# Two more banks for batch 1's key features, weight 1's second half first, and a new order of steps on every engine

## The chip, the cores and the metric

The kernel runs on one core of one Trainium2 chip. The metric is the device time of one execution in microseconds; the number for a kernel is the median of its runs.

## The reference

Polynomial-sketch attention over 4 batches, 4 heads, 1088 tokens and 32 features, followed by a block of layer norm, two matrix products and a residual.

```python
def phi(x):                                   # S1, S2: 8 x 32
    a = np.einsum('rd,bhsd->bhsr', S1, x)
    b = np.einsum('rd,bhsd->bhsr', S2, x)
    return np.einsum('bhsi,bhsj->bhsij', a, b).reshape(*x.shape[:-1], 64)
q_p, k_p = phi(q), phi(k)
kv = np.einsum('bhsf,bhsd->bhfd', k_p, v)     # 64 x 32 for each head
z = np.sum(k_p, axis=2)
num = np.einsum('bhsf,bhfd->bhsd', q_p, kv)
den = np.einsum('bhsf,bhf->bhs', q_p, z)[..., None] + 1e-06
x = (num / den) with the heads side by side   # 4 x 1088 x 128
xn = (x - mu) / np.sqrt(var + 1e-06) * g_ln
out = x + np.maximum(xn @ w_ch1, 0.0) @ w_ch2 # 128 -> 512 -> 128
```

The two weights and the sketches arrive as 64-bit floats; the kernel takes their words apart and builds 32-bit floats from them.

## The kernel before

The kernel has no loops over tiles in its main part. It is a vocabulary of small steps (`k_feat`, `hid`, `store` and so on), each a Python function that issues one to some dozens of instructions, and a string `PROGRAM` that lists 595 steps with their arguments in one order, written out in full. That order is the order of the instructions on each engine. Semaphores follow from the tiles that steps read and write (parts of a tile are kept apart), so an engine that comes to a step whose input is not ready stands still, with everything queued behind it. A letter in a step's arguments names its engine: V is VectorE (DVE), A is ScalarE (ACT), G is GpSimd (POOL), S is SyncE's DMA queue (SP). `store A` is a DMA that is issued from ACT's queue. TensorE (PE) takes `fill`, `bump`, `sk`, `sk_b`, `k_feat`, `k_sum`, `k_sc`, `k_val`, `q_dir`, `q_feat`, `v_flip`, `q_flip`, `f_spr`, `fold`, `num0`, `num`, `hid`, `sec` and `row_pe`. All matmul results go to eight PSUM banks of 512 columns, A, B, C, D, M, N, O and K.

The stages, by batch b (0 to 3) and by chunk c of the block behind it (0 to 7 with 512 tokens each, two for a batch; 8 and 9 with the 128 left-over tokens of two batches):

- `ld*` bring keys, queries, values and weights in. `w_ex`, `w_bits`, `w_exf`, `w_mant`, `w_low`, `w_e2`, `w_e3`, `w_add`, `w_mul` (lines 275 to 342) rebuild the floats of the sketches (0), weight 1 and weight 2; `s_heads` spreads the sketches, and `sk`, `sk_8`, `sk_q`, `sk_qq`, `sk_b`, `sk_2`, `sk_d` prepare them for the matmuls.
- Keys: `turn_g`, `turn_h`, `turn_r` transpose on DVE, `k_feat` (line 507) multiplies with the sketches, `k_tok` (line 517) transposes the result back from PSUM on DVE, `k_prod` (line 82, on POOL or DVE) forms the 64 products in `kp`, `k_sum`, `k_zs` and `k_sc` make the sum z, and `k_val` (line 561) accumulates kv in bank K. There is one `kp` for all batches. `kv_turn`, `kv_wr`, `kv_rd` lay kv out anew through DRAM.
- Queries: `q_feat` (line 629), `q_tok`, `q_ac`, `q_den`, `q_rec`, `q_a2`, `q_prod` (line 82), `q_turn` (line 677), then `num` (line 735) into banks A to D. Half of batch 0 goes another way, `q_dir`, `q_flip`, `f_spr`, `num0` (line 715), whose copies on ACT are `v_cp`, `f_vcp`, `f_rcp` and `q_flcp` (all on line 77). `num_cp` and `num_r` copy to `xT`.
- Block: `hid` (line 843) multiplies 512 columns with a quarter of weight 1, `relu` (line 851 on ACT, 853 on DVE) copies to `hT`, `sec` (line 859) multiplies with weight 2. `row_turn`, `row_wr`, `row_rd` bring x to rows through DRAM, `st_bn` (816), `st_ag` (822) and `st_pow` (827 and 829, on POOL) make the row's 1/std. `fin_a` (878, on ACT) with `fin_g` (888, on POOL), or `fin` (872, on DVE), finish, and `store` writes. The chunks go in the order 0, 1, 2, 3, 8, 4, 5, 6, 7, 9.

`fill` and `bump` are matmuls on a constant into bank M with no reader; they stand in TensorE's order where it has nothing else. `fin_a` issues four activations for a chunk:

```python
    for t in range(tiles(c)):
        act.activation(ob(c)[:, P * t : P * (t + 1)], banks[z][:, P * t : P * (t + 1)],
                       AF.Copy, scale=rstds[slot(c)][:, t : t + 1])
```

Of the kernel before, what the change touches and what calls it, by code (L numbers as in the profile page):

```python
# [24 lines left out]
def kernel(  # L25
# [476 lines left out]
    @op  # L502
    def k_feat(b, u0, u1):
        w = 32 * (u1 - u0)
        for g in range(4):
            for hp in range(2):
                pe.matmul(  # L507
                    X[hp][32 * g : 32 * g + 32, 32 * u0 : 32 * u0 + w],
                    sk8[64 * hp : 64 * hp + 64, :],
                    _ap(kT[b % 2], 64 * hp, 64, 32 * g + P * u0, [[P, u1 - u0], [1, 32]]),  # L510
                    start=True, stop=True, tile_position=(64 * hp, 32 * g),
                )
# [404 lines left out]
    turn_g k 0 0 2; fill 1 128; fill 1 128; sk; ld_g S; turn_r k 0; turn_g k 0 2 4; bump 24;
    sk_8 A; w_e2 A 1 0 256; k_feat 0 0 9; ld S q 1 0 34; w_ex V 1 256 512; w_mant V 1 0 256;
    w_bits V 1 256 512; sk_q; w_add G 1 0 256; fill 1 256; k_tok 0 0 0 9; w_mant A 1 256 512; sk_b;
    k_tok 0 1 0 9; ld_vr S 1 0; fill 1 128; bump 12; w_exf V 1 256 512; k_prod G 0 3 5;  # L920
    turn_h q 0 0; w_e2 A 1 256 512; k_sum 0; fill 4 256; k_zs 0; sk_qq 0; sk_2 A; k_prod G 0 0 3;
    ld_w S 2 0 4; turn_g k 1 0 4; k_sc 0; ld S k 2 0 34; fill 1 256; turn_r q 0; turn_h q 0 1;
    k_sccp A 0; w_low A 1 256 512; k_prod G 0 5 6; ld_v S 1 3; fill 1 128; fill 1 128; k_sccp F 0;
    c_kvb; sk_d; c_pads 1; q_feat 0 4 9; turn_r k 1; w_e3 V 1 0 256; w_e3 V 1 256 512; q_dir 0 4 M;
    w_mul G 1 0 256; q_tok 0 1 4 9; q_tok 0 0 4 9; q_tok 0 2 4 9; w_add G 1 256 512; k_feat 1 0 9;
    q_tok 0 3 4 9; q_cp A 0 4 M 16 24; c_cg V; q_ac G 0 4 9; q_ac0 0 4 M 0; v_flip 1 N;
    k_tok 1 0 0 9; v_flip 2 K; k_prod G 0 6 9; v_flip 0 O; v_flip 3 D; q_den 0 0 4; fold C 0 256;
    v_cp A 2 K; k_tok 1 1 0 9; v_cp A 0 O; v_cp A 3 D; q_rec 0 0 4; turn_r q 1; v_cp A 1 N;
    k_sum 1; q_b0 0 4 M 0; fold_cp A C 0 256; q_den 0 4 9; w_mul G 1 256 512; k_val 0; q_rec 0 4 9;
    q_prod0 2 4 M 0; c_ac 1; w_low A 2 0 512; q_a2 G 0 4 9; sk_qq 2; fold D 256 512; kv_turn 0;  # L930
    q_prod G 0 4 9; q_prod0 0 2 M 0; kv_wr S 0; f_vcp A; q_flip 2 4 1 A; fold_cp A D 256 512;
    q_flip 2 4 0 C; ld_v S 1 2; q_flcp A 2 4 1 A; k_zs 1; f_spr B; q_flip 0 2 0 O; turn_h q 1 1;
    q_flcp A 2 4 0 C; ld_v S 1 1; f_rcp A B; q_flip 0 2 1 D; q_flcp A 0 2 0 O; k_sc 1;
    turn_h q 1 0; ld_vr S 1 1; num0 2 4 N; q_flcp A 0 2 1 D; k_sccp V 1; num0 0 2 O; turn_r k 2;
    k_prod G 1 0 5; num0_cp A 2 4 N; turn_g k 2 0 4; w_bits V 2 0 512; kv_rd S 0; q_feat 1 0 9;
    num0_cp A 0 2 O; ld_v S 1 0; hid O 0 0 0 2; q_tok 1 1 0 9; ld_vr S 2 0; hid N 0 2 2 4;
    q_tok 1 0 0 9; relu A O 0 0 0 2; ld S k 3 0 34; hid M 0 2 0 2; sk_qq 3; ld S q 2 0 34;
    hid K 0 3 0 2; k_prod G 1 5 9; q_tok 1 3 0 9; ld S q 3 0 34; hid B 0 1 2 4; q_tok 1 2 0 9;
    hid D 0 0 2 4; q_turn 4 9; relu A B 0 1 2 4; hid C 0 1 0 2; w_mant A 2 0 512; k_feat 2 0 9;
    relu A K 0 3 0 2; q_ac G 1 4 9; relu A C 0 1 0 2; relu A M 0 2 0 2; q_ac G 1 0 4; k_val 1;  # L940
    k_tok 2 1 0 9; relu A D 0 0 2 4; relu A N 0 2 2 4; k_tok 2 0 0 9; w_ex V 2 0 512; num 0 4 9;
    q_den 1 4 9; k_prod G 2 5 9; w_exf A 2 0 512; q_den 1 0 4; kv_turn 1; q_rec 1 4 9; kv_wr S 1;
    k_sum 2; num_cp A 0 3 4 8; num_cp V 0 1 4 8; num_cp A 0 2 4 8; ld_v S 2 0; hid M 0 3 2 4;
    turn_g k 3 0 4; num_cp A 0 0 4 8; w_e2 A 2 0 512; hid C 1 3 0 4; ld_v S 2 1; w_add G 2 0 512;
    num_r V 0; hid D 1 1 0 4; k_zs 2; w_e3 V 2 0 512; hid O 1 0 0 4; turn_r q 2; turn_h q 2 0;
    kv_rd S 1; w_mul G 2 0 512; hid N 1 2 0 4; turn_r k 3; q_rec 1 0 4; relu A O 1 0 0 4;
    row_turn 1; relu A D 1 1 0 4; q_a2 G 1 4 9; k_sc 2; row_turn 0; k_feat 3 0 9; relu A C 1 3 0 4;
    q_prod G 1 4 9; relu A M 0 3 2 4; row_wr S 0; sec O 0 0; k_tok 3 1 0 9; relu A N 1 2 0 4;
    ld_v S 2 2; turn_h q 2 1; ld_v S 2 3; sec O 0 3; k_sccp V 2; k_tok 3 0 0 9; ld_vr S 2 1;
    turn_r q 3; sec O 0 1; q_a2 G 1 0 4; row_wr S 1; q_turn 4 9; q_prod G 1 0 4; row_rd S 0 0;  # L950
    sec M 1 3; row_rd S 0 2; row_rd S 0 1; sec M 1 1; row_rd S 0 3; k_prod G 2 0 5; q_turn 0 4;
    q_feat 2 0 9; sec M 1 2; q_tok 2 2 0 9; row_rd S 1 2; q_tok 2 1 0 9; row_rd S 1 1; sec O 0 2;
    q_tok 2 3 0 9; ld_v S 3 2; q_tok 2 0 0 9; k_sum 3; ld_v S 3 1; q_ac V 2 4 9; num 1 0 9;
    q_den 2 4 9; ld_vr S 3 1; q_rec 2 4 9; row_rd S 1 3; turn_h q 3 1; row_rd S 1 0; q_ac V 2 0 4;
    k_val 2; q_den 2 0 4; num_r A 1; num_cp A 1 0 0 4; num_cp V 1 1 0 4; num_cp A 1 3 4 8;
    num_cp A 1 3 0 4; row_turn 8; num_cp A 1 2 0 4; num_cp A 1 2 4 8; row_turn 2; num_cp A 1 0 4 8;
    hid M 8 1 0 1; hid N 2 2 0 4; k_zs 3; row_wr S 2; num_cp V 1 1 4 8; k_prod V 3 5 9; row_wr S 8;
    hid C 8 2 0 1; relu A N 2 2 0 4; hid A 2 1 0 4; q_a2 V 2 4 9; hid D 2 3 0 4; st_bn 0;
    relu A A 2 1 0 4; q_rec 2 0 4; hid B 2 0 0 4; relu A D 2 3 0 4; k_sc 3; hid A 8 3 0 1;
    relu A B 2 0 0 4; kv_turn 2; hid D 3 3 0 4; st_ag 0; kv_wr S 2; k_sccp V 3; row_turn 3;  # L960
    st_pow 0; sec N 2 0; row_wr S 3; hid B 3 0 0 4; ld_v S 3 0; q_prod G 2 4 9; relu A M 8 1 0 1;
    relu V A 8 3 0 1; fin_a O 0; ld_vr S 3 0; sec M 1 0; row_rd S 8 1; relu A C 8 2 0 1;
    hid O 8 0 0 1; row_rd S 3 2; relu A B 3 0 0 4; hid K 3 1 0 4; kv_rd S 2; q_a2 G 2 0 4;
    q_turn 4 9; row_rd S 3 3; hid A 3 2 0 4; q_prod G 2 0 4; row_rd S 8 3; sec N 2 1; ld_v S 3 3;
    relu A A 3 2 0 4; turn_h q 3 0; row_rd S 2 2; relu A O 8 0 0 1; relu A D 3 3 0 4; sec N 2 3;
    row_rd S 2 3; k_prod G 3 0 5; q_turn 0 4; relu A K 3 1 0 4; row_rd S 2 0; sec N 2 2;
    row_rd S 2 1; st_bn 1; row_rd S 3 1; q_feat 3 0 9; st_ag 1; sec K 3 2; fin_g G 0;
    q_tok 3 2 0 9; q_tok 3 0 0 9; sec K 3 1; q_tok 3 3 0 9; st_pow 1; q_tok 3 1 0 9; k_val 3;
    q_ac V 3 0 4; q_den 3 0 4; q_rec 3 0 4; q_ac G 3 4 9; fin_a M 1; q_a2 V 3 0 4; num 2 0 9;
    st_bn 2; fin_g G 1; kv_turn 3; q_den 3 4 9; kv_wr S 3; st_ag 2; sec O 8 0; num_cp A 2 3 4 8;  # L970
    num_cp V 2 2 4 8; row_rd S 3 0; num_cp A 2 1 4 8; num_cp A 2 0 4 8; st_pow 2; row_rd S 8 0;
    store A 1 2 0 4; num_cp V 2 0 0 4; sec K 3 0; num_cp V 2 2 0 4; row_turn 5; hid M 5 0 0 4;
    q_rec 3 4 9; q_prod G 3 0 4; row_wr S 5; fin_a N 2; store S 0 2 0 4; sec K 3 3; kv_rd S 3;
    num_r A 2; num_cp A 2 1 0 4; num_cp A 2 3 0 4; hid A 5 2 0 4; row_turn 4; q_a2 G 3 4 9;
# [62 lines left out]
```

## Time and profile before

| what | value |
|---|---|
| median of 3 runs (lowest to highest) | 102.05 us (102.02 to 102.29) |
| the profiled execution's own time | 102.09 us |
| its span, first to last instruction | 100.3 us, so 1.8 us lie around it |
| busy: PE, DVE, POOL, ACT | 95.6, 70.8, 60.7, 40.4 us |
| granted TensorE clock | 1.00 |

All times in the views are microseconds from the start of the span. A busy engine is one that has an instruction under way; matmuls overlap in TensorE's pipeline, and their ends are modelled. The chain follows the work that ended last back from its end, and says at each step which engine and line it was on. In the lists of instructions the columns are the start, the duration, the engine, the line, and the tiles written and read; in the groups by line they are the busy time, the mean duration in ns, and the engine's idle time ahead of them with what ended it. A `xN` is the number of instructions; a 32-bit `hid` or `fill` is two matmul instructions, a `sec` eight.

### The profile page before, as it was taken

How to read it: one execution, taken by the hardware profiler on the slowest of the kernel's cores; microseconds unless marked ns; L12 is line 12 of the kernel's file. 1: busy time of each engine (PE TensorE's matmuls, PEld its weight loads, DVE VectorE, ACT ScalarE, POOL GpSimd, SP SyncE). 2: the span in 40 equal slices, each digit the busy share in tenths (PEclk: the TensorE clock that was granted, in tenths of full speed). 3: DMA queues.
4: the chain of work that ended last, by engine and by line, in shares of the span. 5: the costliest groups of instructions: out<-in, count | busy, mean ns of one | idle time of the engine just before them, and what ended most of it. 6: DMA issues, size and time to landing. Idle time of an engine off the chain costs nothing.

```text
span 100.3 us, 3442 instructions
## 1 busy us (share of the span) xinstructions
PE 95.6 (95%) x1348; PEld 69.5 (69%) x1348; DVE 70.8 (71%) x234; ACT 40.4 (40%) x118; POOL 60.7 (61%) x84
## 2 busy tenths in 40 slices
...
DMA packets 14863, 15.16 MB, mean 151 GB/s; under 512 B 4096, under 2 KB 11136, under 8 KB 14848
## 3 DMA queue, kind: packets, MB, share of 16 engines
...
q14 instruction: 5, 0.04, 0.1%
...
## 4 chain that ended last, share of the span: by engine, by line
PE 93%; ACT 1%; DVE 1%; issue 0%; DVEq 0%
PE bankM L250 9%; PE bankO L859 8%; PE bankK L859 6%; PE bankN L859 6%; PE bankM L859 6%; PE bankD L843 5%; PE bankA L843 5%; PE bankN L843 5%; PE bankK L561 5%; PE bankB L843 4%; PE bankM L843 4%; PE bankC L843 3%; PE bankA L735 3%; PE bankC L859 3%; PE bankO L843 3%; PE bankA L507 2%
## 5 line engine op out<-in xcount | busy, mean ns | idle before, releaser
L82 POOL TENSOR_TENSOR kp<-kf 128x1280 f32<-128x1280 f32 (+4 forms) x9 | 15.7, 1752 | 2.2 <-PE bankK L561 1.6
L827 POOL TENSOR_SCALAR va<-mv 128x4 f32<-128x4 f32 (+1 forms) x10 | 2.3, 227 | 24.4 <-DVE mv L822 15.5
L82 POOL TENSOR_TENSOR qp<-a,fq 128x1280 f32<-128x1280 f32 (+1 forms) x7 | 15.4, 2207 | 0.3
L677 DVE STREAM_TRANSPOSE qpT<-qp 128x1280 f32<-128x1280 f32 (+1 forms) x7 | 9.7, 1384 | 3.8 <-POOL qp L82 3.8
L250 PE MATMUL bankM<-ones 128*128 128x256 f32 (+1 forms) x34 | 10.4, 457 | 1.2 <-DVE top L180 1.2
L829 POOL TENSOR_TENSOR rstd<-va,mhalf 128x4 f32<-128x4 f32 (+1 forms) x10 | 9.4, 943 | 0.8
L250 PEld LDWEIGHTS bankM<-ones 128*128 128x128 f32 x34 | 7.5, 249 | 2.8 <-DVE top L180 1.2
L859 PEld LDWEIGHTS bankO<-w,hT 128*128 128x128 f32 x64 | 7.6, 192 | 1.4 <-issue 0.9
L859 PE MATMUL bankO<-w,hT 128*128 128x128 f32 x64 | 8.4, 280 | 0.0
L859 PEld LDWEIGHTS bankN<-w,hT 128*128 128x128 f32 x56 | 6.9, 192 | 1.4 <-issue 1.0
L859 PEld LDWEIGHTS bankK<-w,hT 128*128 128x128 f32 x56 | 6.9, 192 | 1.4 <-issue 1.4
L859 PE MATMUL bankK<-w,hT 128*128 128x128 f32 x56 | 7.3, 277 | 0.0
L816 DVE BATCH_NORM_STATS2 st<-x 128x6 f32<-128x128 f32 x32 | 6.7, 275 | 0.6 <-DMA x<-xd 0.6
L859 PE MATMUL bankN<-w,hT 128*128 128x128 f32 x56 | 7.1, 275 | 0.0
L797 DVE STREAM_TRANSPOSE xh<-xT 128x512 f32<-128x512 f32 x8 | 5.4, 689 | 2.1 <-ACT xT L77 2.1
L851 ACT ACTIVATE hT<-bankD 128x512 f32<-128x512 f32 (+1 forms) x6 | 3.4, 566 | 7.8 <-PE bankD L843 7.7
L859 PEld LDWEIGHTS bankM<-w,hT 128*128 128x128 f32 x48 | 5.8, 192 | 0.9 <-issue 0.9
L859 PE MATMUL bankM<-w,hT 128*128 128x128 f32 x48 | 6.1, 277 | 0.0
L735 PE MATMUL bankD<-qpT,kvr 32*32 32x288 f32 (+1 forms) x64 | 5.9, 386 | 0.0
L735 PE MATMUL bankC<-qpT,kvr 32*32 32x288 f32 (+1 forms) x64 | 5.9, 386 | 0.0
L735 PE MATMUL bankB<-qpT,kvr 32*32 32x288 f32 (+1 forms) x64 | 5.8, 386 | 0.0
L735 PE MATMUL bankA<-qpT,kvr 32*32 32x288 f32 (+1 forms) x64 | 5.8, 384 | 0.0
(227 smaller groups left out, 247.7 us busy)
## 6 DMA issues: line engine op xcount, KB each, us to landing
...
```

Of the source, the lines that this page charges most:

```text
L82: by[eng].tensor_tensor(out=o, in0=a, in1=b, op=ALU.mult)
L250: pe.matmul(M[0][:, 0:w], ones[:, 0:P], ones[:, 0:w], start=True, stop=True)
L561: pe.matmul(KV[D * h : D * h + D, 0:F], vn[b][:, TW * h + D * u : TW * h + D * (u + 1)], kp[:, H * F * u + F * h : H * F * u + F * (h + 1) ...
L677: dve.transpose(_ap(qpT, 0, P, 32 * u0, [[32, u1 - u0], [TW, 8], [1, 32]]), qp[:, H * F * u0 : H * F * u1])
L735: pe.matmul(X[r][D * h : D * h + D, o : o + w], kvr[b % 2][rows, F * h + D * f : F * h + D * f + D], qpT[rows, c : c + w], start=(f == 0), ...
L797: dve.transpose(_ap(xh[slot(c)], 0, P, 0, [[32, n], [32 * n, 4], [1, 32]]), cols(c))
L816: dve.bn_stats(out=sts[slot(c)][:, 6 * t : 6 * t + 6], in_=row_ap(c, t))
L827: pool.tensor_scalar(out=vas[slot(c)][:, 0:n], in0=_ap(mvs[slot(c)], 0, P, 1, [[2, n]]), scalar1=1e-6, scalar2=None, op0=ALU.add)
L829: pool.tensor_tensor(out=rstds[slot(c)][:, 0:n], in0=vas[slot(c)][:, 0:n], in1=mhalf[:, 0:n], op=ALU.pow)
L843: pe.matmul(banks[z][:, 0:n], w1[:, P * j : P * (j + 1)], cols(c)[:, a : a + n], start=True, stop=True)
L851: act.activation(o, i, AF.Relu)
L859: pe.matmul(banks[z][:, DM * t : DM * (t + 1)], h[:, 512 * j + P * t : 512 * j + P * (t + 1)], w2[:, DM * j : DM * (j + 1)], start=(j == 0 ...
```

## The change

`k_feat` and `k_tok` write and read banks N and O for batch 1, and A and B as before for the others. The program string is another order of 595 steps. TensorE issues the same steps as before (with other letters for many banks), the fills and bumps among them, in another order: `k_feat 1` stands ahead of `q_feat 0`, behind the four fills; `q_feat 1` stands ahead of `num0`; `k_feat 2` and `k_sum 2` come sooner; `k_sum 3` and `k_sc 3` stand ahead of `k_val 2`, and `k_val 2` ahead of `num 1`; chunks 0 and 1 have all but one of their `sec` done before `num 1`. Weight 1's second half is loaded first and its first half third; each batch's loads stand at other places of SP's queue.

Steps that change their engine: `w_add` and `w_mul` of weight 2 from POOL to DVE; `s_heads` from POOL to DVE; `w_e2 0` from DVE to ACT and `w_exf 0` from ACT to DVE; `w_exf` and `w_mant` of weight 1's two halves change places between ACT and DVE; `q_a2 2 4 9`, `q_ac 3 0 4` and `q_a2 3 0 4` from DVE to POOL; of `k_prod 3` the part 0 to 5 is DVE's now and the part 5 to 9 POOL's (before the other way round). DVE has 13 `relu` steps instead of 6. Some `num_cp` and `num_r` change between ACT and DVE, and stores change between ACT's and SP's queues (five more on SP's).

The code, and of the program's diff the new lines (old ones left out) of the opening, of the stretch from `k_val 1` on, and of the stretch round `sec N 2 0`:

```diff
+    def XK(b):
+        return [banks["N"], banks["O"]] if b == 1 else X
...
-                    X[hp][32 * g : 32 * g + 32, 32 * u0 : 32 * u0 + w],
+                    XK(b)[hp][32 * g : 32 * g + 32, 32 * u0 : 32 * u0 + w],
...
-                      X[hp][:, 32 * u0 : 32 * u1])
+                      XK(b)[hp][:, 32 * u0 : 32 * u1])
...
+    w_mant A 1 0 256; fill 1 256; s_heads V; w_exf V 1 0 256; ld S v 0 0 32; fill 1 128;
+    turn_g k 0 2 4; w_add G 1 0 256; w_e2 A 1 0 256; fill 1 128; ld_vr S 1 1; fill 1 128;
+    turn_r k 0; sk; w_mant V 1 256 512; ld_vr S 0 1; fill 1 256; turn_g k 0 0 2; sk_8 A;
+    w_add G 1 256 512; bump 12; ld_vr S 0 0; w_e3 V 1 0 256; k_feat 0 0 9; ld S k 2 0 34; c_cg V;
+    sk_d; w_mul G 1 0 256; bump 24; k_tok 0 0 0 9; k_tok 0 1 0 9; sk_b; turn_h q 0 1; k_sum 0;
+    k_prod G 0 0 3; ld S q 1 0 34; fill 4 256; k_zs 0; ld_w S 2 0 4; turn_g k 1 0 4; sk_q; sk_2 A;
+    k_prod G 0 5 6; turn_r k 1; turn_r q 0; turn_h q 0 0; k_sc 0; sk_qq 0; k_feat 1 0 9;
+    k_prod G 0 6 9; k_sccp A 0; w_exf A 1 256 512; k_sccp F 0; fill 1 128; w_e2 A 1 256 512;
+    k_tok 1 1 0 9; q_feat 0 4 9; k_tok 1 0 0 9; q_dir 0 4 O; q_tok 0 2 4 9; w_e3 V 1 256 512;
...
+    num_cp A 0 2 4 8; relu A N 0 1 0 2; w_e3 V 2 0 512; w_low A 2 0 512; hid C 1 3 0 4; kv_turn 1;
+    q_den 1 4 9; kv_wr S 1; k_zs 2; w_add V 2 0 512; hid M 1 0 0 4; ld_v S 2 0; relu A C 1 3 0 4;
+    q_rec 1 0 4; ld_v S 2 2; w_mul V 2 0 512; num_r A 0; q_a2 G 1 0 4; hid N 1 2 0 4; ld_v S 2 3;
+    relu A M 1 0 0 4; q_rec 1 4 9; row_turn 1; q_a2 G 1 4 9; hid D 1 1 0 4; k_prod G 2 5 9;
...
+    q_a2 G 2 4 9; q_prod G 2 4 9; sec N 1 1; num_cp A 1 0 4 8; num_cp V 1 3 4 8; num_cp A 1 2 4 8;
+    q_den 2 0 4; num_cp A 1 1 4 8; num_cp A 1 0 0 4; num_cp V 1 3 0 4; num_cp A 1 2 0 4;
+    num_cp A 1 1 0 4; hid K 3 3 0 4; num_r A 1; row_turn 2; q_rec 2 0 4; hid D 3 0 0 4; row_wr S 2;
+    turn_h q 3 1; ld_v S 3 1; q_a2 G 2 0 4; row_turn 3; hid O 8 2 0 1; q_prod G 2 0 4; ld_v S 3 2;
+    relu A D 3 0 0 4; hid B 2 3 0 4; row_turn 8; st_bn 0; relu A K 3 3 0 4; ld_v S 3 3;
+    hid D 3 1 0 4; ld_vr S 3 0; st_ag 0; kv_rd S 2; turn_h q 3 0; hid C 2 0 0 4; row_wr S 8;
+    st_bn 1; ld_v S 3 0; hid A 3 2 0 4; relu A C 2 0 0 4; st_ag 1; relu A D 3 1 0 4; turn_r q 3;
+    hid K 2 1 0 4; k_prod V 3 0 5; st_pow 1; relu A B 2 3 0 4; relu A A 3 2 0 4; hid C 2 2 0 4;
+    st_pow 0; relu V K 2 1 0 4; fin_a N 1; sec O 3 2; row_rd S 8 1; q_turn 4 9; relu A C 2 2 0 4;
+    row_wr S 3; sec O 3 3; fin_g G 1; fin_a M 0; row_rd S 8 3; q_turn 0 4; sec N 2 0; row_rd S 8 0;
...
```

In the old program the four steps behind `k_val 2` on TensorE were `hid M 8 1`, `hid N 2 2`, `hid C 8 2` and `hid A 2 1`; `k_prod V 3 5 9` stood on DVE between `num_cp V 1 1 4 8` and `q_a2 V 2 4 9`, with POOL's `st_pow 0` behind DVE's later `st_bn 0` and `st_ag 0`.

More of the change, by code (lines that the diff above doesn't have):

```diff
@@ L917 @@
[L917 to L974, printed above, removed]
-    q_turn 0 4; row_wr S 4; q_prod G 3 4 9; hid B 4 2 0 4; relu A A 5 2 0 4; store A 1 3 0 4;
-    row_rd S 5 0; row_rd S 5 1; hid N 5 1 0 4; st_bn 3; relu A B 4 2 0 4; store A 1 1 0 4;
```

99 lines of the change are left out of this document (68 added, 31 removed).

## The prediction

> **What bounds the kernel now.** I read the page first, then busy time by stretches, then the chain.
>
> ```profile
> span 100.3 us, 3442 instructions
> PE 95.6 (95%) x1348; PEld 69.5 (69%) x1348; DVE 70.8 (71%) x234; ACT 40.4 (40%) x118; POOL 60.7 (61%) x84
> PE 93%; ACT 1%; DVE 1%; issue 0%; DVEq 0%
> ```
>
> TensorE is busy nearly throughout, and 93% of the chain lies on it. The profiled execution took 102.09 us, 1.8 more than its span and 0.04 more than the median of 102.05. The change issues the same TensorE steps, fills included, so it has no matmul to save: it can win only where TensorE stands still now, and loses wherever the new order makes it stand. Where it stands:
>
> ```profile
> PEld bankN L715 <- ACT kvb L77: 0.3, 1, 0.3
> PEld bankK L561 <- ACT vn L77: 0.3, 1, 0.3
> PE bankK L561 <- ACT vn L77: 0.2, 1, 0.2
> PEld bankO L715 <- ACT v L77: 0.2, 1, 0.2
> ```
>
> These rows of the waits are 1.0 us: 0.5 in `k_val 0`, which waits for the `v_cp` copies, and 0.5 in the two `num0`, which wait for `f_rcp` and `q_flcp`. The chain gives the places and the prices of the steps:
>
> ```profile
> 1.19 5.46 PE bankM L250 x14
> ...
> 7.53 0.40 PE bankA L507
> ...
> 9.93 0.19 PE bankK L532 x16
> ...
> 22.45 0.63 PE bankO L843 x2
> ...
> 42.96 1.14 PE bankK L561 x72
> ...
> 44.52 0.86 PE bankN L843 x2
> 45.38 0.22 PE bankC L843 x2
> ...
> 49.48 0.89 PE bankN L859 x8
> ```
>
> From the first `hid` at 22.45 to the last `sec` no wait of TensorE over 0.3 us is in the list. A `hid` costs 0.86, one of a left-over tile 0.22, a `sec` 0.89.
>
> **The opening, up to `k_sum 0`.** The same fills and bumps stand ahead of `k_sum 0` in both orders (six fills of 256, three of 128, 36 bumps). The first seven take 5.46 us. What is new is who decides when `k_feat 0` starts:
>
> ```profile
> 7.01 0.44 ACT L410 ACTIVATE sk<-bankK,m 128x16 f32<-128x16 f32 x2 [1.69 <-PE bankK L374]
> 7.33 0.51 ACT L310 ACTIVATE exf<-exf,m 128x256 f32<-128x256 f32 x1
> 7.87 0.51 ACT L311 ACTIVATE ex<-exf,top 128x256 uint32<-128x256 f32 x1
> ```
>
> Now `sk_8` runs at 7.01 and `w_e2` follows it; then `w_e2` (two times 0.51) stands ahead of `sk_8` on ACT, and a third fill of 128 ahead of `sk` on TensorE. I put `k_feat 0` at about 8.2 instead of 7.53. More than half of that is filler moved ahead of it, which is saved behind it; what is left is `k_sum 0` about 0.2 later (bounds 0 and 0.7). The new load order costs nothing as long as DVE has other weight work ahead of `turn_g k 0 0 2`, which it has.
>
> **From `k_sum 0` to the first `hid`.** Both orders hold five fills of 256 and two of 128 here; the new one holds `k_feat 2` besides, which the old one runs later. The two waits of `num0` should go: `f_spr` now has `q_feat 1` behind it, and that covers ACT's copies. At `k_val 0` the last `v_cp` still comes late, since what stands between (one fill, a fold, `k_sc 1`) is about as long as before; I keep 0.3 of the 0.5. `k_feat 2` may wait up to 0.2 for DVE's `q_tok 1 0`. Gain: 0.5 + 0.2 - 0.2 (opening) = 0.5 us, bounds -0.3 and 1.0.
>
> **`k_val 1` to `num 1`.** Weight 2's `w_add` and `w_mul` are DVE's now, and `q_rec 1 4 9` is queued behind them. POOL waits for it before `q_a2`, `k_prod 2 5 9`, both `q_prod 1`, `sk_qq 2` and `k_prod 2 0 5`, which `k_val 2` needs.
>
> ```profile
> L82 POOL TENSOR_TENSOR qp<-a,fq 128x1280 f32<-128x1280 f32 x4 | 9.6, 2397 | 0.2
> L82 POOL TENSOR_TENSOR qp<-a,fq 128x1024 f32<-128x1024 f32 x3 | 5.9, 1953 | 0.2
> 32.73 0.46 POOL L82 TENSOR_TENSOR a<-fq,rden 128x160 f32<-128x160 f32 x1
> 38.02 2.39 POOL L82 TENSOR_TENSOR kp<-kf 128x1280 f32<-128x1280 f32 x1
> 30.64 0.71 DVE L318 SCALAR_TENSOR_TENSOR bits<-w_raw,ex 128x512 uint32<-128x512 uint32 x1 [0.35 <-ACT ex L311]
> ```
>
> That is 2 x 2.40 + 2 x 1.95, 0.46 for `q_a2` and 0.2 for `sk_qq`, 9.4 us. TensorE has four `hid` (3.4), seven `sec` (6.2) and some 2.3 of small steps (an estimate for `k_feat`, `q_feat`, `k_sum` and two `k_sc`) between `k_val 1` and `k_val 2`: about 12. So `q_rec` must come within 2.6 us of `k_val 1`'s end. Behind that end DVE has `kv_turn`, a `q_den`, `k_zs`, the two weight steps and the `q_rec`: about 2.4 by my estimate (the weight steps at 0.6 each, half of the 1.20 of the 1024-wide product below). It fits with 0.2 to spare. The cost I take is 0; it is 1.0 if `w_e3` (0.71) and one more copy are still ahead.
>
> **Round `sec N 2 0`.** Here I expect the change to lose. First, two rows of what DVE and POOL do to each other:
>
> ```profile
> L282 DVE TENSOR_SCALAR bits<-w_raw 128x256 uint32<-128x256 uint32 x2 | 0.6, 282 | 0.0
> 22.02 1.15 DVE L282 TENSOR_SCALAR bits<-w_raw 128x512 uint32<-128x512 uint32 x1
> 20.49 2.38 POOL L82 TENSOR_TENSOR kp<-kf 128x1280 f32<-128x1280 f32 x1
> 22.82 0.39 POOL L425 COPY skq<-skq 128x16 f32<-128x16 f32 x1
> 17.99 0.20 POOL L425 COPY skq<-skq 128x16 f32<-128x16 f32 x1
> ```
>
> The 512-wide `w_bits` took 1.15 where twice the 256-wide one is 0.56. It started under POOL's product, which ended at 22.87, and ended 0.3 behind that; POOL's next copy then took 0.39 instead of 0.20. I read this as: each stood still while the other ran. The Trainium skill ("SBUF — State Buffer", section "Who interferes with whom") states it as a rule: a port pair that VectorE and GpSimd share is held for a whole instruction, and a VectorE instruction with two SBUF inputs takes it against a GpSimd instruction that reads SBUF. The trace agrees for `w_bits` (1.15 against 0.56).
>
> The new program puts `k_prod V 3 0 5`, a product of two SBUF operands, on DVE right behind `st_ag 1`, whose result POOL's `st_pow 1` takes. `fin_a N 1` on ACT waits for `st_pow 1`; `relu C 2 2` is queued behind it on ACT; `sec N 2 0` needs both. The prices:
>
> ```profile
> 43.31 0.31 DVE L797 STREAM_TRANSPOSE xhr<-xTr 128x128 f32<-128x128 f32 x1
> 43.99 0.71 DVE L797 STREAM_TRANSPOSE xh<-xT 128x512 f32<-128x512 f32 x1 [0.37 <-ACT xT L77]
> 44.90 1.20 DVE L82 TENSOR_TENSOR kp<-kf 128x1024 f32<-128x1024 f32 x1
> 46.26 0.86 DVE L816 BATCH_NORM_STATS2 st<-x 128x6 f32<-128x128 f32 x4
> 48.53 0.34 DVE L822 BATCH_NORM_AGGREGATE mv<-st 128x2 f32<-128x6 f32 x4
> L457 DVE STREAM_TRANSPOSE qT<-qn 128x512 f32<-128x512 f32 x8 | 5.3, 673 | 0.0
> L827 POOL TENSOR_SCALAR va<-mv 128x4 f32<-128x4 f32 x8 | 1.8, 227 | 22.2 <-DVE mv L822 13.4 <-DVE skq L554 8.5
> L829 POOL TENSOR_TENSOR rstd<-va,mhalf 128x4 f32<-128x4 f32 x8 | 8.3, 1035 | 0.7
> 50.34 1.14 ACT L878 ACTIVATE ob<-bankO,rstd 128x128 f32<-128x128 f32 x4
> L851 ACT ACTIVATE hT<-bankC 128x512 f32<-128x512 f32 x2 | 1.2, 601 | 0.3 <-PE bankC L843 0.3
> ```
>
> From the end of `num 1`: ACT's copies until `row_turn 2` 1.1 (43.99 - 42.96, and one copy more); on DVE `row_turn` twice (1.42) and the small one (0.31), `turn_h` twice (1.34), `st_bn` twice (1.72), `st_ag` twice (0.68): 6.6, less some 0.5 because neighbours overlap, 6.1. `k_prod` of 1280 is 1.25 x 1.20 = 1.5. If it takes the port first, `st_pow 1` starts at 7.6 and takes 0.23 + 1.03 and a gap of 0.1, to 9.0; `fin_a` 1.14, `relu` 0.60: `sec N 2 0` can start at 10.8. TensorE gets there after `sec N 1 1` (1.0), eight `hid` (6.9), one small (0.2) and two `sec` (1.8): 9.9. It stands still for 0.9 us. If `st_pow` goes first, the result is there at 9.3 and nothing is lost. Bounds 0 and 1.3; I take 0.9.
>
> **The rest.** Behind that, products, stores and `fin` stand in another order, but TensorE still has the same end, one `sec`, one `fin`, two stores. I cost it at 0; a store's landing holds `fin C 8 0` on DVE with `relu N 4 0` behind it, which the eight `hid` ahead of `num 3` cover; uncovered it would be some tenths.
>
> **Sum.** 102.05 - 0.5 + 0.9 = 102.45, as 102.4 us. From no change a measurement of this kernel can tell about 0.3%, 0.3 us.
>
> **Rivals.** *The stall does not come* (POOL gets its turn between `st_ag 1` and `k_prod`, or ACT is early): the gain of the first half is kept, 102.05 - 0.5 = 101.55 us, faster. For it: the rest of the walk finds no other wait over 0.2. Against: `k_prod` needs nothing that comes later than `st_ag`. It decides by the order at the port: with `k_prod` starting 0.3 us behind `st_pow`'s second instruction's start it is this case.
>
> *Weight 2 on DVE makes POOL late as well*: `k_prod 2 0 5` ends about 0.8 behind TensorE's reaching `k_val 2`, on top of the forecast: 102.45 + 0.8 = 103.25 us. For it: the slack is 0.2 in 12 us, where now the product ends at 40.41 and `k_val 2` starts at 42.96. Against: POOL is rid of two 128x512 steps.
>
> *The order does nothing*: the opening eats its gain (0.7 later instead of 0.2) and the stall is hidden by that: 102.05 us.
>
> **How the numbers follow.** Forecast 0.42, its own range 102.0 to 102.9; no stall 0.30; POOL late 0.22; nothing 0.06. Faster by over 0.3%: 0.27 of the second and 0.04 of the first, 0.31. Within 0.3%: 0.12 + 0.03 + 0.03, 0.18. Slower: 0.26 + 0.22 + 0.03, 0.51. The range goes from the second case with 0.35 more gain (of the 0.5 to its bound), 101.2, to a little over the third, 103.4.
>
> **What would show it.** Right: in the changed profile TensorE's waits name no ACT line 77 at line 715; `w_e2` runs ahead of `sk_8`; the 1280-wide `k_prod` on DVE overlaps a long `va` or `rstd` of POOL, and the first `sec` of chunk 2 waits for an ACT `hT`. Wrong: no wait of TensorE over 0.3 behind 22 us (then it is faster), or a wait of `k_val 2` for POOL's `kp`, or waits at places I cost at nothing.

## The result, and the profile after

The changed kernel takes 103.88 us (median of six runs, 102.96 to 104.52) against 102.03 us for the kernel before on the same chip (101.88 to 102.58): a ratio of 1.0136, 95% interval 1.0092 to 1.0181. The profiled execution took 104.25 us, 1.8 around its span of 102.5. One of these six executions, and some of those below, is slow (over 1.5% above the fastest of its kernel); ratios leave such executions out, and the profiled executions of the fifth and the ninth kernel below are two of them, so their traces are read for who waits for whom. The page of the kernel after:

```profile
span 102.5 us, 3437 instructions
PE 96.9 (95%) x1348; PEld 70.2 (69%) x1348; DVE 72.4 (71%) x241; ACT 38.1 (37%) x112; POOL 60.1 (59%) x84
PE 88%; DMA 4%; DVE 2%; ACT 1%; issue 1%; ACTq 0%
```

The second and third of these lines are the reading: TensorE has the same 1348 matmuls, but it holds only 88% of the chain instead of 93, and 4% are now a transfer. Busy time by stretches shows where. The columns are the stretch, its length, then busy time and instructions of PE, PEld, DVE, ACT and POOL, clock, DMA share, GB/s. First the kernel before, then the kernel after, from 66 to 76 us:

```profile
66.00:76.00 10.00, 10.00 (x102) 5.78 (x101) 6.28 (x24) 6.53 (x18) 7.03 (x8) 1.00 0.49 138
```

```profile
66.00:76.00 10.00, 9.14 (x88) 4.24 (x87) 6.91 (x20) 4.13 (x11) 4.26 (x6) 1.00 0.49 140
```

TensorE has 14 matmuls fewer in these 10 us and stands still for 0.86 of them; ACT is busy for 4.13 us instead of 6.53 (in the whole second half of the span for 14.55 instead of 16.82, since the change gave `relu` steps to DVE). The waits of TensorE after (engine, tile and line, whom it waits for, us in total, times, longest), leaving out those that the kernel before has too:

```profile
PEld bankK L846 <- DVE hT L856: 1.2, 1, 1.2
PEld bankD L738 <- ACT hT L854: 1.0, 1, 1.0
PEld bankA L510 <- DVE fq L642: 0.6, 1, 0.6
PE bankD L738 <- ACT hT L854: 0.4, 1, 0.4
PE bankK L846 <- DVE hT L856: 0.4, 1, 0.4
```

Line 846 is `hid K 5 3`, 738 is `num 3`, 510 is `k_feat 2`. Matmul by matmul, `hid D 5 2` (up to the start of `hid K 5 3`) takes 0.58 more than 0.86 and `num 3` takes 2.87 instead of 1.53. Together that is 1.9 of the 2.16 us by which the two profiled executions differ. This stretch, `hid D 5 2`, `hid K 5 3` and `num 3`, is called the round below: it takes 5.40 us, where the last two `hid` ahead of `num 3` and `num 3` itself take 3.35 in the kernel before. Of the rest, `sec O 3 3` and `sec N 2 0` are 0.4, and the stretch up to the first `hid` gains 0.13 (`k_feat 2` counted in both).

The chain after, at this place (start, duration, what):

```profile
68.08 4.30 DMA kvr<-xdk
...
72.41 0.32 ACTq L896
...
72.78 1.09 ACT hT L854 x2
...
75.47 1.09 PE bankM L862 x8
```

And the instructions of ACT and DVE there:

```profile
68.53 4.20 ACTq L896 DMA_DIRECT2D out_dram<-ob  x4
72.78 0.60 ACT L854 ACTIVATE hT<-bankM 128x512 f32<-128x512 f32 x1 [3.65 <-DMA out_dram<-ob]
...
67.65 0.29 DVE L819 BATCH_NORM_STATS2 st<-xr 128x6 f32<-128x128 f32 x1 [2.12 <-DMA out_dram<-ob]
...
70.72 0.65 DVE L856 TENSOR_SCALAR hT<-bankK 128x512 f32<-128x512 f32 x1
```

ACT issues four stores (A 0 0, A 1 0, A 2 0, A 2 1) from 68.53 to 72.73, and `relu A M 4 1` behind them starts 3.65 us after ACT's last work, with `relu A D 5 2` and so `num 3` behind it. The single issues show why it takes so long: the third goes at 70.41, when POOL's `fin_g G 2` has ended; the fourth at 72.41. The transfers of both queues take eight semaphores, called slots below, in turn (the landings in this trace name eight), and each issue waits until the transfer eight before it has landed; for the fourth store that is `kv_rd 3`, which SP issued at 68.08 (64.85 in the kernel before) and which landed at 72.39, 0.02 ahead of the issue. DVE has its own version: `st_bn 8` stands still for 2.12 us until `row_rd 8 2` has landed (the row names a store, but the wait of the same instruction is put down to `xr<-xd` in the first and the second kernel below), and `relu V K 5 0`, which holds `hid K 5 3`, is queued behind it. Of `fin_g G 2` it is the first cause as well, since POOL does `st_pow 8` ahead of it.

The place that the prediction had named, `sec N 2 0`:

```profile
50.10 1.45 DVE L85 TENSOR_TENSOR kp<-kf 128x1280 f32<-128x1280 f32 x1
50.14 1.51 POOL L830 TENSOR_SCALAR va<-mv 128x4 f32<-128x4 f32 x1 [1.35 <-DVE mv L825]
52.81 1.14 ACT L881 ACTIVATE ob<-bankN,rstd 128x128 f32<-128x128 f32 x4 [1.04 <-POOL rstd L832]
```

The product is 0.04 us ahead of POOL, and POOL's `va` takes 1.51 instead of 0.23. That `va` is held under the product is as forecast; it cost 0.4, not 0.9.

### The profile page after: what moved, and what is told of

It reads as the page before. It is cut to its first block, busy times and chain, and to the rows that moved or that the text cites. A ratio compares the mean times of both kernels' runs of the same rounds, so it can differ in the third digit from the quotient of the medians.

```text
span 102.5 us, 3437 instructions
## 1 busy us (share of the span) xinstructions
PE 96.9 (95%) x1348; PEld 70.2 (69%) x1348; DVE 72.4 (71%) x241; ACT 38.1 (37%) x112; POOL 60.1 (59%) x84
## 4 chain that ended last, share of the span: by engine, by line
PE 88%; DMA 4%; DVE 2%; ACT 1%; issue 1%; ACTq 0%
PE bankN L862 11%; PE bankM L253 9%; PE bankM L862 5%; PE bankK L564 5%; PE bankD L862 4%; PE bankC L862 4%; DMA kvr<-xdk 4%; PE bankO L846 4%; PE bankD L846 4%; PE bankO L862 4%; PE bankB L846 3%; PE bankK L846 3%; PE bankM L846 3%; PE bankC L846 3%; PE bankN L846 3%; PE bankA L738 2%
## 5 line engine op out<-in xcount | busy, mean ns | idle before, releaser
L85 POOL TENSOR_TENSOR kp<-kf 128x1024 f32<-128x1024 f32 (+4 forms) x9 | 15.3, 1704 | 0.8 <-DVE kf L520 0.8
L830 POOL TENSOR_SCALAR va<-mv 128x4 f32<-128x4 f32 (+1 forms) x10 | 3.6, 358 | 19.1 <-DVE mv L825 18.8
L862 PEld LDWEIGHTS bankN<-w,hT 128*128 128x128 f32 x88 | 10.9, 191 | 3.0 <-issue 2.8
L862 PE MATMUL bankN<-w,hT 128*128 128x128 f32 x88 | 12.0, 281 | 0.0
L85 POOL TENSOR_TENSOR a<-fq,rden 128x160 f32<-128x160 f32 (+1 forms) x7 | 3.4, 488 | 6.7 <-DVE rden L662 3.9
L862 PEld LDWEIGHTS bankC<-w,hT 128*128 128x128 f32 x40 | 5.1, 192 | 1.4 <-issue 1.0
L891 POOL TENSOR_TENSOR ob<-ob,x 128x512 f32<-128x512 f32 x4 | 5.1, 1275 | 1.6 <-ACT ob L881 1.6
L846 PE MATMUL bankD<-xT,w 128*128 128x512 f32 (+1 forms) x12 | 5.7, 557 | 0.0
L80 ACT COPY xT<-bankA 128x128 f32<-128x128 f32 x6 | 1.6, 275 | 10.1 <-PE bankD L738 10.1
L862 PE MATMUL bankC<-w,hT 128*128 128x128 f32 x40 | 5.3, 275 | 0.0
```

Source lines behind the costliest of these rows:

```text
L85: by[eng].tensor_tensor(out=o, in0=a, in1=b, op=ALU.mult)
L830: pool.tensor_scalar(out=vas[slot(c)][:, 0:n], in0=_ap(mvs[slot(c)], 0, P, 1, [[2, n]]), scalar1=1e-6, scalar2=None, op0=ALU.add)
L846: pe.matmul(banks[z][:, 0:n], w1[:, P * j : P * (j + 1)], cols(c)[:, a : a + n], start=True, stop=True)
L862: pe.matmul(banks[z][:, DM * t : DM * (t + 1)], h[:, 512 * j + P * t : 512 * j + P * (t + 1)], w2[:, DM * j : DM * (j + 1)], start=(j == 0 ...
L891: by[eng].tensor_tensor(out=o, in0=o, in1=i, op=ALU.add)
```

## The experiments

All kernels change the program's order only, unless said. In the diffs the steps of other engines in between are left out. Ratios are to the kernel before on the same chip, with the 95% interval. The changed kernel itself came to 1.0136 above and to 1.0212 in a later measurement (the fifteenth): ratios from different measurements that lie closer together than this 0.8% do not tell two kernels apart.

**First: two stores behind the relu.**

```diff
-    store A 2 0 0 4; store A 2 1 0 4; relu A M 4 1 0 4; relu A D 5 2 0 4; relu A K 5 3 0 4;
+    relu A M 4 1 0 4; relu A D 5 2 0 4; relu A K 5 3 0 4; store A 2 0 0 4; store A 2 1 0 4;
```

> The changed kernel with ACT's stores A 2 0 and A 2 1 moved behind relu A K 5 3. Theory (the two stores hold ACT, first for POOL's fin_g G 2, then for a slot that the transfer kv_rd 3 still holds, and relu D 5 2 behind them holds num 3): relu M 4 1 starts at about 69.4 instead of 72.78, num 3 takes 1.5 to 1.7 us instead of 2.87, the time falls by 1.1 to 1.4 us to 102.5 to 102.8. It is then kv_rd 3's own landing (72.4) that num 3 meets. Rival (DVE is what is late: st_bn 8 waits 2.1 us, relu K 5 0 behind it holds hid K 5 3 by 0.58): ACT is free earlier, num 3 still waits, time within 0.3 of the changed kernel's. Second rival (the loss is spread over many small waits): at most 0.3 faster.

103.51 us, ratio 1.0137 (1.0094 to 1.0181): no gain that can be told, though ACT did what the theory said (`relu A M 4 1` at 69.55 instead of 72.78). `num 3` still took 2.56. Its chain:

```profile
68.64 4.23 DMA out_dram<-ob
...
73.11 0.36 DVE ob L875
...
73.51 0.43 PE bankC L738
```

`num 3` waited 0.6 us for `kv_rd 3`'s landing, as expected, but a second lock (a wait that holds `num 3` by itself) lay behind the first: `fin C 8 0` on DVE (line 875) writes the output buffer that chunk 0 had, waits until `store A 0 0` has landed, and holds bank C, which `num 3` needs. The transfer took 4.23 us.

**Second: batch 3's kv earlier on SP's queue.**

```diff
-    kv_turn 3; store S 0 3 0 4; row_wr S 4; row_rd S 3 3; kv_wr S 3; row_rd S 8 2; kv_rd S 3;
+    kv_turn 3; kv_wr S 3; store S 0 3 0 4; row_wr S 4; kv_rd S 3; row_rd S 3 3; row_rd S 8 2;
```

> The changed kernel with kv_wr 3 issued right behind kv_turn 3 and kv_rd 3 ahead of row_rd 3 3 on SP's queue; the stores stay on ACT. Theory (the store waits for the slot that kv_rd 3 holds): with kv_rd 3 issued at about 64 and landed by 68, store A 2 1 goes at about 70.8, behind store A 2 0 which still waits for POOL; relu M 4 1 starts at about 71 instead of 72.78, num 3 loses its wait, 1.0 to 1.4 us faster. Rival (the ACT wait is for POOL's fin_g 2, or for a store's own data): relu M 4 1 still starts at about 72.7, no gain over 0.3.

104.31 us, 1.019 (1.015 to 1.023): not better. `num 3` had no wait (1.53), but `row_rd 8 2` stood behind one more transfer, `st_bn 8` started 0.6 us later (counted from `k_sum 0`), and TensorE waited for the same DVE relu as before, for longer:

```profile
65.55 3.22 DMA xr<-xd
...
68.86 0.30 DVE st L819
...
72.19 0.66 DVE hT L856
...
72.90 1.12 PE bankK L846 x2
```

The rival was right on ACT: `relu A M 4 1` at 72.50 waited for `fin_g G 2`, which is late by `st_bn 8` too.

**Third: the product behind a relu.**

```diff
-    k_prod V 3 0 5; relu V K 2 1 0 4;
+    relu V K 2 1 0 4; k_prod V 3 0 5;
```

> The changed kernel with DVE's k_prod V 3 0 5 moved behind relu V K 2 1. Theory of the prediction's fourth step (the product holds the port, st_pow 1 stretches to 1.51 us and fin_a N 1 and relu C 2 2 come late): va takes 0.23 to 0.4 us, fin_a N 1 starts about 1 us earlier, the waits of sec O 3 3 and sec N 2 0 go, 0.3 to 0.4 us faster by the trace, 0.9 by the prediction. Rival (the stall there has another cause, or is given back at the wait ahead of num 3): va short, time within 0.2 of the changed kernel's, since the later wait for the transfer and the stores doesn't move with TensorE.

103.65 us, 1.0139 (1.01 to 1.0177). POOL and ACT:

```profile
50.43 0.23 POOL L830 TENSOR_SCALAR va<-mv 128x4 f32<-128x4 f32 x1 [1.35 <-DVE mv L825]
51.91 1.17 ACT L881 ACTIVATE ob<-bankN,rstd 128x128 f32<-128x128 f32 x4
```

`va` is back at 0.23, `fin_a N 1` comes 1.2 us sooner, counted from `num 1`, and `sec O 3 3` and `sec N 2 0` are 0.29 shorter on TensorE. The time does not show it, and could hardly: 0.29 us is less than the interval tells. `num 3` takes 2.87 again, but the gain is not given back there in this trace, where the round takes 5.12 us.

**Fourth: the first two, and `row_rd 8 2` early.**

```diff
+    row_rd S 2 2; row_rd S 8 2;
...
-    kv_wr S 3; row_rd S 8 2;
```

> The changed kernel with the two stores behind relu A K 5 3, kv_wr 3 and kv_rd 3 early, and row_rd 8 2 issued behind row_rd 2 2, so that st_bn 8 does not wait. Theory: both losses of that round go (1.34 at num 3, 0.58 at hid K 5 3): 1.7 to 2.0 us faster than the changed kernel, 101.9 to 102.2, level with the kernel before. Rival (spread over small waits): at most 0.5 faster.

103.22 us, 1.0072 (1.0039 to 1.0105). DVE's wait is gone (`hid D 5 2` 0.86, `hid K 5 3` 0.95), `num 3` still takes 2.93:

```profile
66.14 4.51 DMA x<-xd
...
70.72 1.79 DMA out_dram<-ob
...
72.65 0.36 DVE ob L875
```

Now `store A 0 0` finds its semaphore held by a `row_rd` of 4.51 us, goes at 70.72, and `fin C 8 0` waits for it. The other lock is not open either: `relu A D 5 2`, behind this store and the next on ACT, ends at 73.25, 0.24 behind `fin C 8 0`.

**Fifth and sixth: chunk 8 with an output buffer of its own.** The fourth kernel with this, and all four stores behind `relu A K 5 3`; the sixth has the third's edit too.

```diff
     obs = const([P, 512], F32, "ob", 4)
+    ob8 = const([P, P], F32, "ob8")
...
-        return obs[order.index(c) % len(obs)]
+        return ob8 if c == 8 else obs[order.index(c) % len(obs)]
```

> The changed kernel with the transfers of the fourth kernel (kv_wr 3 and kv_rd 3 early, row_rd 8 2 early), all four of ACT's stores A 0 0, A 1 0, A 2 0, A 2 1 behind relu A K 5 3, and an output buffer of its own for chunk 8, so that fin C 8 0 waits for no store of chunk 0. Theory (the round ahead of num 3 is held by stores: ACT by their slots, DVE's fin C 8 0 and so bank C by store A 0 0's landing): num 3 takes 1.5 to 1.7 us instead of 2.9, hid D 5 2 and hid K 5 3 0.86 each, 1.0 to 1.4 us faster than the fourth kernel's 103.0 to 103.2, that is 101.8 to 102.2. Rival (the round is bound by the DMA engines themselves, by landings of 4 us; whatever is moved, something that TensorE needs lands late): another wait of 0.8 us or more ahead of num 3 or sec M 4 1, and 102.7 to 103.2.

> The fifth kernel with DVE's k_prod V 3 0 5 behind relu V K 2 1 as in the third. Theory (once num 3's round has no wait, TensorE's gain of 0.3 us at sec O 3 3 and sec N 2 0 is no longer given back): 0.2 to 0.4 us faster than the fifth kernel, 101.5 to 101.9, a little under the kernel before. Rival (given back at another wait, as the third kernel's was to a part): within 0.15 of the fifth kernel.

Sixth: 102.47 us, 1.0035 (1.0011 to 1.0058). `num 3` takes 1.62, both `hid` are clean, and the stretch reads as before:

```profile
66.00:76.00 10.00, 10.00 (x105) 6.13 (x104) 7.83 (x23) 5.73 (x17) 4.38 (x6) 1.00 0.54 154
```

Fifth: 103.97 us, 1.0169 (1.0141 to 1.0197), worse than expected, and 1.5 more than the sixth. Its `num 3` took 1.89, but the four stores held ACT again, now ahead of batch 3's copies; DVE's copy of bank D follows ACT's, and `hid M 9 0` on TensorE (line 847 here) waits for it:

```profile
74.51 3.88 ACTq L897 DMA_DIRECT2D out_dram<-ob  x4
78.43 0.27 ACT L80 COPY xT<-bankD 128x128 f32<-128x128 f32 x1 [3.39 <-DMA out_dram<-ob]
78.73 0.19 DVE L82 COPY xTr<-bankD 128x32 f32<-128x32 f32 x1 [1.79 <-ACT xT L80]
PE bankM L847 <- DVE xTr L82: 0.7, 1, 0.7
```

In the sixth the same four took 1.79. The slots that the last three waited for in the fifth are those of `row_rd 5 1`, `store S 2 3` and `row_rd 5 0`, which landed at 75.89, 76.60 and 77.98. Laid side by side, the fifth's trace has 0.25 us more at the product, 0.27 at `num 3` and 1.02 behind `sec M 4 1`, which is the 1.5 between the two times. The reading has a limit: this execution took 106.11 us, 2.1 above the median, and lost the 2 us ahead of `k_val 0`, so that its transfers met TensorE at other moments than in the other five; and why they land later against TensorE than in the sixth is open.

**Seventh: batch 1's key features in the old banks.**

```diff
-        return [banks["N"], banks["O"]] if b == 1 else X
+        return X
```

In this order `q_feat 0` overwrites bank A ahead of `k_tok 1 0`: this kernel leaves out the wait that would keep half of batch 1's key features. It waits for `k_tok 1 1` alone, not for both as the expectation has it, and one that kept them would wait longer.

> The changed kernel with batch 1's key features in banks A and B again; the order is the changed one. Theory (the two banks are what lets q_feat 0 follow k_feat 1 at once): q_feat 0 has to wait for both k_tok 1 on DVE, until about 14.0 instead of 13.36 us, and TensorE is 0.5 to 0.7 us later from there to the first hid. Rival (the loss meets later waits, of k_val 0, q_feat 1 and k_feat 2 for DVE, and goes into them): at most 0.2 later at the first hid, and the time within 0.3 of the changed kernel's.

104.82 us, 1.0285 (1.0259 to 1.0311). From `k_sum 0` to the first `hid` it takes 13.51 us instead of 12.97: `q_feat 0` and `v_flip 3` lose 0.3 each. So the two banks are worth 0.54 in this order by the trace, as the first theory said, and more in a kernel that keeps the keys; by the times it is 0.4 to 0.9 (against 103.88 and 104.44 of the changed kernel).

**Eighth: `k_feat 2` behind the first `hid`.**

```diff
-    k_feat 2 0 9; hid N 0 1 2 4;
+    hid N 0 1 2 4; k_feat 2 0 9;
```

> The changed kernel with k_feat 2 moved behind hid N 0 1 2 4 on TensorE. In the changed kernel k_feat 2 starts 0.25 to 0.3 us late, since q_tok 1 0 on DVE still reads bank A. Theory (k_feat 2's place costs that, and hid N could run in the meantime): hid N starts at the end of num0, at 22.0 to 22.3, k_feat 2 has no wait, the stretch up to hid M is 0.2 to 0.3 us shorter, as the prediction's second step had it. Rival (k_feat 2 was cover: hid N then waits for num0_cp on ACT, which ends at 22.66): hid N waits as long as k_feat 2 did, no gain over 0.1.

105.33 us, 1.031 (1.0285 to 1.0334). The rival, and more of it:

```profile
PEld bankN L846 <- ACT xT L80: 1.0, 1, 1.0
PE bankN L846 <- ACT xT L80: 0.6, 1, 0.6
```

`hid N` waits for ACT's `num0_cp`; the stretch from `k_sum 0` to `hid M` is 0.56 longer. `k_feat 2` was the cover of that copy, with its own wait of 0.3.

**Ninth and tenth: the keys' loads first.** The changed kernel, and the sixth, with

```diff
-    ld_w S 1 0 2; ld S k 0 16 34; ld S k 0 0 16;
+    ld S k 0 16 34; ld S k 0 0 16; ld_w S 1 0 2;
...
+    turn_g k 0 0 2; w_ex V 1 0 256; w_bits V 1 0 256; w_exf V 1 0 256;
+    sk_8 A; w_low A 1 0 256; w_mant A 1 0 256; w_e2 A 1 0 256; w_add G 1 256 512; w_add G 1 0 256;
+    k_tok 0 1 0 9; w_e3 V 1 0 256;
+    k_prod G 0 5 6; w_mul G 1 0 256;
```

> The changed kernel with both loads of batch 0's keys ahead of the second-loaded half of weight 1 (ld_w 1 0 2), as the kernel before has it, and with that half's steps on DVE behind turn_g k 0 0 2, on ACT behind sk_8, its w_e3 and w_mul behind k_tok 0 1 and k_prod 0 5 6. Eight profiles of kernels with the changed opening had k_sum 0 at 9.93 to 10.55 us, mean 10.2, against 9.74 in the one profile of the kernel before, and k_feat 0 waited there for DVE's kT and ACT's sk. Theory (two weight loads ahead of the keys make the keys land late, and the steps ahead of turn_g k 0 0 2 and sk_8 add to it): kT is done by 7.4 instead of 7.9 to 8.7, k_sum 0 starts at 9.5 to 9.8, 0.4 us faster. Rival (TensorE's own fillers set it, as the prediction's first step had it with 0.2): k_sum 0 stays at 9.9 to 10.2, and the time within 0.2.

> The sixth kernel (stores behind relu, transfers of batch 3 early, own output buffer for chunk 8, product behind relu) with the opening of the ninth. If the losses of the change are the opening (0.4), the port (0.3) and the round ahead of num 3 (1.3 to 1.9), this kernel has none of them, and comes to 101.9 to 102.2 us, level with or a little under the kernel before. Rival (the opening's gain is met by a later wait): 102.3 to 102.6 as the sixth kernel.

105.20 us, 1.0234 (1.0166 to 1.0302), and 102.96 us, 1.0018 (0.9979 to 1.0056). `k_sum 0` came at 9.60 and 9.46, as the theory had it, and the edit then lost more than it gained: from `k_sum 0` to `k_val 0` both take 8.70 us instead of 7.25, 1.2 of it in one wait. In the tenth:

```profile
9.49 2.27 POOL L85 TENSOR_TENSOR kp<-kf 128x768 f32<-128x768 f32 x2
9.64 1.63 DVE L321 SCALAR_TENSOR_TENSOR bits<-w_raw,ex 128x256 uint32<-128x256 uint32 x1 [0.23 <-ACT ex L314]
12.95 0.30 PE L549 MATMUL bankK<-zT,s2b 128*128 128x32 f32 x1 [1.19 <-ACT s2b L401]
```

The moved `w_e3` fell under POOL's product and took 1.63 where it takes 0.38 to 0.55 elsewhere in the profiles of the changed order; `k_zs` on DVE, `sk_2` on ACT and `k_sc 0` on TensorE followed.

**Eleventh: one part alone in the kernel before**, banks N and O and

```diff
-    q_feat 0 4 9; turn_r k 1; k_feat 1 0 9; k_tok 1 0 0 9; k_tok 1 1 0 9;
+    turn_r k 1; k_feat 1 0 9; k_tok 1 0 0 9; k_tok 1 1 0 9; q_feat 0 4 9;
```

> The kernel before with one part of the change alone: batch 1's key features in banks N and O, and turn_r k 1, k_feat 1 and both k_tok 1 ahead of q_feat 0. Theory (the part is a filler moved, and only the waits of k_val 0 and num0 could pay for it): DVE's q_tok 0 come 0.9 to 1.2 us later behind the two k_tok 1, the v_flip and q_ chain behind them too; 0.2 to 0.8 us slower than the kernel before. Rival (the part carries the change's gain of 0.3 in that stretch by itself): 0.2 to 0.4 faster. Either way not the 1.4% that the whole change costs.

103.65 us, 1.0114 (1.0073 to 1.0154): slower, as the theory said, by more than its 0.8. `v_flip 0` and `v_flip 3` are 0.8 longer, since DVE's `q_tok 0` come behind both `k_tok 1`; the part pays only with the order around it.

**Twelfth: the kernel before once more.**

> The kernel before once more, for a second profile. If the opening's loss belongs to the change, k_sum 0 starts at 9.6 to 9.9 again and no row has k_feat 0 waiting for DVE's kT; if it is only how far the loads' landings scatter, it starts at up to 10.4 here too. Its num 3 is expected at 1.53 us without a wait.

102.18 us, `num 3` 1.53, and the chain at `k_feat 0`:

```profile
7.59 0.40 PE bankA L507
```

`k_sum 0` started at 9.80 (9.74 in the first profile). The eight profiles with the changed opening had it at 9.93 to 10.55, so the later opening seemed to belong to the change; a later one, the seventeenth's, has 9.61, so it does so on the average and not each time.

**Thirteenth, fourteenth, fifteenth: the opening again, without the product above it.** The ninth's and tenth's edit, with `w_e3 V 1 0 256` behind `w_e3 V 1 256 512`, and `w_mul G 1 0 256` and `c_kvb` behind `k_prod G 0 3 5`; and the changed kernel itself.

> The ninth kernel (the changed kernel with the keys' loads ahead of the second-loaded half of weight 1), with that half's w_e3 on DVE behind w_e3 1 256 512, where POOL is idle, and its w_mul with c_kvb on POOL behind k_prod 0 3 5. Theory (the opening costs the change 0.4 to 0.5 on the average, by the keys' landing): w_e3 takes 0.4, k_sum 0 starts at 9.5 to 9.7, k_sc 0 at 11.3 to 11.7 without the wait of 1.2, and the time is 0.3 to 0.6 under the fifteenth kernel's. Rival (a later wait takes it, at k_val 0 or at num 3, whose transfers do not come sooner with TensorE): within 0.2 of the fifteenth.

> The sixth kernel (stores behind relu, batch 3's transfers early, own output buffer, product behind relu) with this opening. Theory (opening 0.45, port 0.3 and the round ahead of num 3 1.3 to 1.9 are the whole loss): 101.4 to 101.9 us, 0.2 to 0.6% under the kernel before. Rival (the opening's gain is taken by a later wait): 102.2 to 102.6, as the sixth.

> The changed kernel once more, on the chip of the two above and for a second profile. If the round ahead of num 3 is the loss and no accident of one execution: num 3 takes 2.4 to 2.9 us again, with relu on ACT or fin C 8 0 on DVE as what it waits for, hid D 5 2 or hid K 5 3 0.4 to 0.6 longer than 0.86, and the time is 1.2 to 1.8% over the kernel before. If it was an accident: num 3 at 1.5 to 1.7.

103.78 us, 1.0138 (1.0101 to 1.0175); 102.02 us, 0.9982 (0.9962 to 1.0001); 104.44 us, 1.0212 (1.0173 to 1.0251). In the thirteenth `k_sum 0` starts at 9.60, but `v_flip 3 N` then waits 0.3 for DVE's `q_tok`, and `k_val 0` starts at 17.30, inside the 16.9 to 17.9 of the profiles with the changed opening: the trace is for the rival, the times (0.66 less than the fifteenth) for the theory. `k_val 0` starts at 17.46 on the average of ten profiles with the changed opening (the fifth's left out) and at 17.24 in the three with the keys first, so I leave the opening's worth between 0.2 and 0.7. The fifteenth has the same round, 4.66 us with `num 3` at 2.65, through all three locks at once:

```profile
PEld bankK L846 <- DVE hT L856: 0.8, 1, 0.8
PEld bankC L738 <- DVE ob L875: 0.5, 1, 0.5
PEld bankD L738 <- ACT hT L854: 0.4, 1, 0.4
```

The fourteenth, with every lock opened, is level with the kernel before: 0.2% under it, with an interval that still touches no change.

**Sixteenth and seventeenth: the four stores where ACT has nothing behind them.** The fourteenth kernel, and the changed kernel with the own buffer alone, with

```diff
-    store A 0 0 0 4; store A 1 0 0 4; store A 2 0 0 4; store A 2 1 0 4;
...
-    fin_a O 3;
+    fin_a O 3; store A 0 0 0 4; store A 1 0 0 4; store A 2 0 0 4; store A 2 1 0 4;
```

> The fourteenth kernel with the four stores A 0 0, A 1 0, A 2 0, A 2 1 behind fin_a O 3 instead of relu A K 5 3. In the fourteenth they took 2.82 us on ACT, num_cp of batch 3 behind them came 2.3 us late, and sec K 5 3 and hid M 9 0 lost 0.15 and 0.25 by it. Theory (a store waits for its slot wherever it stands, and holds what is behind it): with nothing behind them, num_cp starts at once, those 0.4 us come back, 101.5 to 101.8 us, 0.4 to 0.7% under the kernel before. Rival (the stores' data buffers or their landings are then what fin of chunks 4 and 5 waits for): a wait of DVE's fin later, no gain, 102.0 or more.

> The changed kernel with only the four stores behind fin_a O 3 and chunk 8's own output buffer, which that needs; SP's order, the product and the opening are the changed ones. If the stores are the greater part of the round's loss: hid K 5 3 keeps its 0.2 to 0.6 (DVE, by row_rd 8 2), num 3 waits only for kv_rd 3's landing at about 72 (0 to 0.6), 1.0 to 1.5 us faster than the changed kernel, 102.6 to 103.0. Rival (the transfers that land late are the cause, the stores only one of those that wait for them): num 3 still takes 2.3 us or more and the time is within 0.5 of the changed kernel's.

Seventeenth: 102.95 us, 1.0072 (1.0048 to 1.0097). The stores alone are about half or more of the loss; `num 3` takes 1.69, `hid K 5 3` keeps its wait for DVE (1.51 us), and what `num 3` meets is what was expected:

```profile
PE bankA L738 <- DMA kvr<-xdk: 0.5, 1, 0.5
```

Sixteenth: 102.29 us, 1.0005 (0.9981 to 1.003), no better than the fourteenth: `sec M 4 1` now waits 0.3 for DVE's `relu V N 4 0`, queued behind `st_bn 3` and its rows. No kernel here beats the kernel before by more than can be told.

## Why the prediction was right and wrong

The direction was right, the size was not: 0.4 us forecast, 1.85 measured, beyond the upper end of the range. The direction was luck in the main: the two terms that the prediction priced came to 0.26 us in the profiled execution (0.39 lost at `sec N 2 0`, 0.13 gained ahead of the first `hid`), less than a measurement tells from no change, and the rest came from a term priced at nothing.

- *The rest, costed at 0*: this is the step that failed. It holds 1.9 of the 2.16 us of the profiled execution, and the later kernels show it: the round takes 5.40 us in the changed kernel (4.66 in its second profile), 4.05 in the seventeenth with the stores and the shared buffer out of the way, 3.42 and 3.34 in the sixth and the fourteenth with the kv transfers and `row_rd 8 2` moved too, and 3.35 in the kernel before. The times follow: 1.0136 and 1.0212, then 1.0072, then 1.0035 and 0.9982 (the last two with the product's edit, the fourteenth with the opening's as well). The fifth stands apart: 1.0169 with a round of 3.70, since its stores held batch 3's copies behind it. The prediction did name `fin C 8 0` behind a store's landing, and said that eight `hid` cover it. In the changed kernel itself the covered lock was not the last one (`fin C 8 0` ended at 72.75, `relu A D 5 2` at 73.86); in the first kernel it was, with a landing of 4.23 us, and `num 3` needs the very bank that `fin C 8 0` reads. Such landings are in the trace before as well, where other transfers crowd (five `x<-xd` that were issued there between 52.4 and 56.2 us took 4.4 us in the median, against 2.1 of all 32). The prediction did not look at all at the four stores in a row on ACT's queue ahead of three `relu`, nor at `kv_rd 3`, which has ten transfers between `kv_turn 3` and itself on SP's queue besides its `kv_wr 3`, where the kernel before has four. Both could be read from the two programs.
- *Round `sec N 2 0`*: mechanism right, size wrong. The third kernel gives 0.29, the trace 0.4, against 0.9. The chain of durations held to within 0.4 us (`fin_a` at 52.81, 8.8 behind `num 1` instead of 9.0), but `relu C 2 2` overlapped the end of `fin_a`, and `sec N 2 0` starts on its first two quarters of `hT` while the third is still being made.
- *`k_sum 0` to first `hid`*: 0.32 gained where 0.7 stood against the opening's 0.2. The two terms were sized the wrong way round: `k_val 0` gave 0.44 and not 0.2, but the two `num0` with what follows gave 0.06 and not 0.5. Their waits for ACT went, as forecast; `k_feat 2` behind them then waits for `q_tok`. The eighth kernel shows that one step later is no better place for it.
- *The opening*: 0.2 in the profiled execution, as forecast; over ten profiles (the fifth's left out) `k_sum 0` starts at 10.12 on the average (9.61 to 10.55), 0.35 later than in the two of the kernel before. The sentence that the new load order costs nothing was wrong: two weight loads ahead of the keys make `kT` late, and `k_feat 0` waits for it (1.02 us in the second kernel, 0.43 in the seventeenth).
- *POOL late at `k_val 2`*, the rival: it did not happen; `k_val 2` has no wait.
- *The shared port*: the tenth kernel met it a second time, from the other side. In the first case POOL took 1.51 us against 0.23, in the second DVE 1.63 against 0.38 to 0.55. The rule of the Trainium skill ("SBUF — State Buffer", section "Who interferes with whom") is that a VectorE instruction with two SBUF inputs and a GpSimd instruction that reads SBUF contend for a shared port pair, which is an exclusive lock; both cases agree with it. The `w_bits` that the prediction set beside the rule has one SBUF input (`bits<-w_raw`), so its 1.15 us shows that one engine stood still under the other, and not the part on two inputs.
